# One output in three thirds: the channel mix of the first 256 tokens, with new order tables

## The chip, the cores and the metric

The kernel runs on one core of a Trainium2 chip. A core has a matrix engine (TensorE, PE in the profile), three engines for elementwise work (VectorE or DVE, ScalarE or ACT, GpSimd or POOL) and a queue engine (SyncE or SP) that issues most DMA transfers. Each engine takes its own instructions strictly in the order in which they were written; engines wait for each other by semaphores. The metric is the time of one execution on the device in microseconds; lower is better.

## What is computed

Three layers stand one behind the other, for 4 batches of 576 tokens and a width of 512. In the reference, cut to what matters:

```python
# attention, 8 heads of 64, causal in blocks of 64 tokens
scores = np.where(mask, scale * np.matmul(q, k.transpose(0, 1, 3, 2)), -1e9)
attn = np.exp(scores - np.max(scores, axis=-1, keepdims=True))
attn = attn / (np.sum(attn, axis=-1, keepdims=True) + 1e-09)
x = np.matmul(attn, v)                        # heads side by side: (4, 576, 512)
# channel mix
xk = mu_k * x + (1.0 - mu_k) * x_prev         # x_prev: x shifted by one token
xr = mu_r * x + (1.0 - mu_r) * x_prev
k = np.maximum(xk @ w_k, 0.0)                 # (512 -> 1024)
v = k * k @ w_v                               # (1024 -> 512)
x = 1.0 / (1.0 + np.exp(-(xr @ w_r))) * v     # w_r: 512 -> 512
# token and channel mixer
u = x + (np.maximum(x.transpose(0, 2, 1) @ w_tok1, 0.0) @ w_tok2).transpose(0, 2, 1)
out = u + np.maximum(u @ w_ch1, 0.0) @ w_ch2
```

## The kernel before, in words

A dense product is made of numbers split into an upper and a lower part, each of which TensorE multiplies exactly enough: w·x becomes wh·xh + wl·xh + wh·xl, three matmuls in place of one. Weights are split where they arrive, chunk by chunk, by `load_split`: a DMA loads a chunk (L345), ACT casts its top (L352), DVE joins (L355), ACT makes the upper part (L361) and POOL the lower part (L364). Chunks of w_r and w_k come first, those of w_v while the first batch is at work.

Work is cut into groups. `a{b}{hf}{pr}` is the attention of batch b, half hf and head pair pr; half 0 is the first 256 tokens (two blocks of 128 queries, j = 0 and 1), half 1 the other 320 (j = 2, 3 and, of 64 queries, 4). A unit of such a group and one j goes through scores (PE, L510), largest and bias (DVE, L544 and L553), exponentials (ACT, L563), their sums and inverse (DVE), the upper 16-bit part of the probabilities (`first`, ACT L587) and the lower (`second`, DVE L593), which both go to a tile pin, a transposing DMA on SP's queue (`turn`, L599), which makes the tile pt, and the products with v (`pv.products`, PE L646). Each pt tag, pt0 to pt4 for j = 0 to 4, has two buffers; where j < 4 a unit takes both, one for each head.

`c{b}{hf}` is the channel mix of one half. For each 128 of the 512 channels `mix` scales the shifted tokens (ACT L720), adds the others (DVE L726), and makes the upper part xh (L732, ACT or DVE) and the lower part xl (L736, POOL or DVE). Four `r_group`s, eight `k_group`s and four `v_group`s follow on PE: in an r or k output 8 matmuls with xh (both parts of the weight, L751) and then 4 with xl (L756), in a v output 16 and 8 with kh and kl. They add up in an accumulator of tag l, of which there are two; it comes free when `r_out` (ACT L792), `k_out` (ACT L820) or `v_out` (DVE) has read it. Squares of k are split into kh and kl (L845, L848). Before, all steps of an output wait for both parts of its weights (`need`) and for the parts of x that they read.

Then the last layer follows in groups `f{b}` and `b{n}` (L764 and others); its matmuls fill TensorE from about 400 us on.

The order of all of this is not that of the code. `Plan.schedule` lets each engine choose, among the steps that its model says are ready, the one with the smallest key; a step's key is its due time, less a number for its kind (table `lead_of`), less one for its group (table `shift`), and for the groups of the beginning (`begin`: the weights and the first batch's attention and mix) less one more for its kind (table `lead_begin`). The instructions are then written in that order.

## Time and profile before

| | us |
|---|---|
| median of 3 runs | 805.56 |
| lowest and highest run | 805.19, 806.23 |
| the profiled execution | 811.06 |
| its span, first to last instruction | 809.3 |
| busy in the span: PE | 763.7 |
| DVE | 477.3 |
| ACT | 419.2 |
| POOL | 181.3 |

The times are those of runs without the profiler, apart from the profiled execution, which was taken once and from which all views come. Its mean granted TensorE clock is 0.993 of full speed. The page divides the span in 40 slices; PE is busy 90% or more in nearly all slices but the first few and the last, and the other engines are busy half of the time and more in the first 400 us and little after that. How much of an engine's busy time matters is decided by stretches, and by what ended each wait, so the views by window and the timelines of single engines are used below. In a timeline a row joins like instructions that follow each other (x8); its second number is the time from the start of the first to the end of the last, and the number in brackets is the idle time ahead of it and what ended that.

### The profile page before, as it was taken

To read this page: it belongs to the slowest core of one execution; us is meant where nothing else is said; L and a number is where in the kernel's file an instruction comes from. 1 tells how busy PE (TensorE), PEld (TensorE's weight loads), DVE (VectorE), ACT (ScalarE), POOL (GpSimd) and SP (SyncE) were. 2 spreads that over 40 slices of the span, in tenths; PEclk is the share of its full clock that TensorE was granted. 3 is DMA by queue.
4 is the path that set the end of the run, shared out by engine and by line. 5 is a ranking of instruction groups with operands and counts; after the bars stand their busy time and mean duration, and the time that the engine had idled before them with its cause. 6 is when DMAs were issued, how large, how long until landed. Compare 5 with 4: busy or idle time off the path is not lost.

```text
span 809.3 us, 16129 instructions
## 1 busy us (share of the span) xinstructions
PE 763.7 (94%) x6120; PEld 661.7 (82%) x6120; DVE 477.3 (59%) x1194; ACT 419.2 (52%) x1070; POOL 181.3 (22%) x209
## 2 busy tenths in 40 slices
PE   2459999998999999999999999999999999999998
PEld 1227899887989999999999989998888888888886
DVE  7897898997798987789555687612212302301210
ACT  6887978687678795778564565502201201301100
POOL 3433524334145142432443222200000000000000
PEclk9999999999899999999999999999999999999999
DMA  8976964686465843566552654200000010000001
GB/s 272 269 189 106 201 148 115 146 170 120 113 138 125 159 117 93 117 140 113 191 180 84 232 170 141 78 27 1 14 26 1 14 39 14 1 26 14 14 13 40
DMA packets 136750, 84.30 MB, mean 104 GB/s; under 512 B 110944, under 2 KB 118240, under 8 KB 136160
## 3 DMA queue, kind: packets, MB, share of 16 engines
q1 hardware_dynamic: 136672, 83.27, 41.8%
q8 instruction: 48, 0.79, 0.4%
q14 instruction: 30, 0.25, 0.1%
HBM read 47.58 MB, written 9.44 MB: 70 GB/s over the span
## 4 chain that ended last, share of the span: by engine, by line
PE 81%; DVE 7%; DMA 5%; ACT 5%; issue 2%; SPq 0%; POOL 0%; ACTq 0%; DVEq 0%
PE b L764 37%; PE l L751 18%; PE l L756 9%; PE s L510 5%; PE o L646 4%; PE b L938 3%; PE b L959 3%; DMA pt<-pin 3%; DVE pin L593 2%; DMA wst<-in_w_k 1%; PE b L914 1%; DVE nm L544 1%; ACT pin L587 1%; ACT p L563 1%; DMA qkl<-in_w_v 1%
## 5 line engine op out<-in xcount | busy, mean ns | idle before, releaser
L1030 ACT ACTIVATE wy<-b 128x512 fp32r<-128x512 f32 (+1 forms) x60 | 33.3, 555 | 211.8 <-PE b L764 211.2
L764 PE MATMUL b<-uh,wx 128*128 128x512 f32 (+1 forms) x480 | 139.6, 373 | 0.0
L751 PE MATMUL l<-xh,wx 128*128 128x256 f32 (+1 forms) x768 | 123.7, 302 | 2.2 <-ACT r L792 1.8
L751 PEld LDWEIGHTS l<-xh,wx 128*128 128x128 f32 x768 | 107.9, 190 | 7.4 <-ACT r L792 2.0
L764 PE MATMUL b<-wy,c2a 128*128 128x512 f32 (+1 forms) x460 | 110.8, 367 | 0.0
L764 PEld LDWEIGHTS b<-uh,wx 128*128 128x128 f32 x480 | 87.2, 188 | 17.3 <-issue 0.2
L764 PEld LDWEIGHTS b<-wy,c2a 128*128 128x128 f32 x460 | 79.2, 189 | 15.3
L593 DVE SCALAR_TENSOR_TENSOR pin<-p,rs,pin 128x128 f16<-128x128 f32 (+4 forms) x112 | 77.0, 707 | 7.5 <-ACT pin L587 7.3
L1045 DVE TENSOR_TENSOR x<-b,x 128x256 f32<-128x256 f32 (+7 forms) x32 | 13.5, 454 | 114.8 <-PE b L764 114.8
L751 PE MATMUL l<-kh,wy 128*128 128x256 f32 (+1 forms) x512 | 78.1, 304 | 0.2 <-DVE ve L428 0.2
L646 PEld LDWEIGHTS <-vb 128*64 128x64 f16 x1920 | 52.9, 115 | 29.8 <-issue 13.7
L646 PE MATMUL o<-pt,vb 128*64 128x128 f16 (+1 forms) x1920 | 62.4, 220 | 14.3 <-DMA pt<-pin 7.2
L764 PE MATMUL b<-gx,wx 128*128 128x512 f32 x192 | 75.4, 393 | 0.0
L751 PEld LDWEIGHTS l<-kh,wy 128*128 128x128 f32 x512 | 71.5, 194 | 2.5 <-issue 1.4
L563 ACT ACTIVATE p<-s,nb 128x384 f32<-128x384 f32 (+4 forms) x112 | 61.6, 553 | 19.2 <-DVE nb L553 9.7
L587 ACT ACTIVATE pin<-p,rs 128x128 f16<-128x128 f32 (+4 forms) x112 | 63.2, 588 | 13.2 <-DMA pt<-pin 6.9
L756 PE MATMUL l<-xl,wx 128*128 128x320 f32 (+1 forms) x384 | 68.2, 300 | 0.0
L544 DVE TENSOR_REDUCE nm<-s 128x2 f32<-128x256 f32 (+4 forms) x80 | 63.6, 798 | 1.9 <-PE s L510 1.3
L756 PEld LDWEIGHTS l<-xl,wx 128*128 128x128 f32 x384 | 56.6, 190 | 2.1 <-issue 1.2
L1033 DVE SCALAR_TENSOR_TENSOR wy<-b,wy 128x512 fp32r<-128x512 f32 (+1 forms) x28 | 16.1, 576 | 62.8 <-ACT wy L1030 62.7
L1033 DVE SCALAR_TENSOR_TENSOR gx<-b,wy 128x512 fp32r<-128x512 f32 x32 | 21.9, 690 | 47.8 <-ACT wy L1030 47.8
L736 POOL TENSOR_TENSOR xl<-mt,xh 128x256 fp32r<-128x256 f32 (+1 forms) x32 | 28.4, 891 | 91.7 <-DVE xh L732 52.5
(116 smaller groups left out, 1397.0 us busy)
## 6 DMA issues: line engine op xcount, KB each, us to landing
wst<-in_w_c SPq DMA_DIRECT2D x24, 256.0 KB, 2.7
qkf<-in_kq SPq DMA_DIRECT2D x12, 480.0 KB, 3.5
v<-in_v SPq DMA_DIRECT2D x16, 320.0 KB, 3.1
x<-xd SPq DMA_DIRECT2D x4, 1152.0 KB, 7.0
wst<-in_w_c2a SPq DMA_DIRECT2D x18, 256.0 KB, 2.7
qkl<-in_w_v SPq DMA_DIRECT2D x16, 256.0 KB, 3.4
wst<-in_w_k SPq DMA_DIRECT2D x9, 410.0 KB, 5.4
qkf<-in_kq SPq DMA_DIRECT2D x12, 256.0 KB, 2.9
```

Of the source, the lines that this page charges most:

```text
L510: self.nc.tensor.matmul(o, q[e, q0:q0 + P], k[e, k0:k1], start=n == 0, stop=n == len(terms) - 1)
L544: nc.vector.tensor_reduce(out=c["nm"][:, :nh], in_=m, axis=AX.XY if j == 4 else AX.X, op=ALU.max, negate=True)
L563: nc.scalar.activation(out=c[x], in_=s, func=AF.Exp, scale=0.125, bias=c["nb"][:, x:x + 1], accum_out=c["sm"][:, x:x + 1],)
L587: nc.scalar.activation(out=like(pin[:, :n]), in_=c[x], func=AF.Copy, scale=rs)
L593: nc.vector.scalar_tensor_tensor(out=like(pin[:, w:w + n]), in0=c[x], scalar=rs, in1=like(pin[:, :n]), op0=ALU.mult, op1=ALU.subtract)
L646: nc.tensor.matmul(o[hh * D:hh * D + D, q0:q0 + rows], v[:, i, y, hh, :], st["pt", hh, j][:, x * (j + 1) + i, :], start=i == x == y == 0, ...
L736: (nc.vector if i in pl["xl_d"] else nc.gpsimd).tensor_tensor(out=l, in0=x[i], in1=raw(x["h"][i]), op=ALU.subtract)
L751: self.nc.tensor.matmul(ps, ww[:, k, :], x[0][k], start=k == 0 and n == 0, stop=False)
L756: self.nc.tensor.matmul(ps, w[0][:, k, :], x[1][k], start=False, stop=k == kt - 1)
L764: self.nc.tensor.matmul(ps, ww[k], xx[k], start=k == 0 and n == 0, stop=k == kt - 1 and n == 2)
L1030: nc.scalar.activation(out=gh(m), in_=d["g", m][:, :n], func=AF.Relu)
L1033: nc.vector.scalar_tensor_tensor(out=gl(m), in0=d["g", m][:, :n], scalar=0.0, in1=raw(gh(m)), op0=ALU.max, op1=ALU.subtract)
```

## The change

In group c00, the channel mix of the first 256 tokens of the first batch, every r, k and v output is made in three thirds, each a step of its own: wh·xh, wh·xl and, last, wl·xh. A third waits only for its own part of the weight and its own part of the input (`need` with `parts`). Before, wh·xh and wl·xh were interleaved and wh·xl came last. The number of matmuls is the same. All other groups are made as before.

```diff
+    def mm_one(self, ps, w, x, term, k0, k1, kt):
+
+        ww, xx = ((w[0], x[0]), (w[0], x[1]), (w[1], x[0]))[term]
+        for k in range(k0, k1):
+            self.nc.tensor.matmul(
+                ps, ww[:, k, :], xx[k], start=term == 0 and k == 0, stop=term == 2 and k == kt - 1
+            )
...
-            def r_group(i, k0, k1, xr=xr, c=c, n=n):
-                if k0 == 0:
+            def r_group(i, k0, k1, term=None, xr=xr, c=c, n=n):
+                if k0 == 0 and not term:
                     c["rp", i] = self.ps_l.tile([P, 512], F32, tag="l", name="l")
                 ps = c["rp", i][:, :n]
-                if k0 < KD:
+                if term is not None:
+                    self.mm_one(ps, self.wr[i], (xr["h"], xr["l"]), term, k0, k1, KD)
+                elif k0 < KD:
...
+            begin = b == 0 and hf == 0
+
+            def group(key, fn, i, x, name, ps):
+                if begin:
+                    for term in range(3):
+                        last = step("PE", c_pe(4 * n, 4), key, fn, i, 0, KD, term,
+                                    r=x["tl" if term == 1 else "th"] + self.need(name, i, (term // 2,)), w=[ps])
+                    return last
+                tok = self.need(name, i)
...
-                for k0 in range(0, NF + 1, 4):
+                for term, k0 in itertools.product(range(3), (0, 4)) if begin else ():
+                    step("PE", c_pe(4 * n, 4), key, v_group, i, k0, k0 + 4, term, after=[last],
+                         r=[(tkl if term == 1 else tkh, k) for k in range(k0, k0 + 4)] +
+                         self.need("wv", i, (term // 2,)), w=[ps])
+                for k0 in () if begin else range(0, NF + 1, 4):
...
     shift={
-        "a000": 194.57, "a001": -21.47, "a002": 2.43, "a003": 144.84, "a010": -1.55, "a011": -11.09, "a012": 1.1,
+        "a000": 194.57, "a001": -19.98, "a002": -5.02, "a003": 152.8, "a010": 1.41, "a011": -11.22, "a012": 1.1,
```

The functions `k_group` and `v_group` are changed like `r_group`. The tables `lead_of`, `shift` and `lead_begin` have new numbers, for nearly all kinds and groups, so the order changes on every engine from the first tens of microseconds to the end of attention and mix; from about 400 us on it is nearly the same. Three places show how.

On ACT, at the first `r_out`: l_864 and, after, l_779 are the accumulator of the first r output, qkl_731 and qkl_721 the same chunk of w_v. Before:

```order
L732 CAST xh_805<-mt_721 128x256
L720 ACTIVATE mt_854<-xt0_133,omu_62 128x256
L352 CAST tw1_64<-qkl_731 128x256
L361 CAST wy_72<-qkl_657 128x256
L655 ACTIVATE xt1_593<-o_742,vo_183 128x320
L720 ACTIVATE mt_878<-xt0_131,omu_62 128x256
L792 ACTIVATE r_891<-l_864 128x256
L563 ACTIVATE p_897,sm_896<-s_703,nb_893 128x384
```

After:

```order
L720 ACTIVATE mt_774<-xt0_135,omu_62 128x256
L720 ACTIVATE mt_784<-xt0_131,omu_62 128x256
L563 ACTIVATE p_788,sm_787<-s_707,nb_776 128x384
L361 CAST wy_72<-qkl_664 128x256
L587 ACTIVATE pin0_90<-p_702,rs_710 128x384
L802 ACTIVATE r_811<-l_779 128x256
L352 CAST tw1_64<-qkl_721 128x256
L563 ACTIVATE p_821,sm_787<-s_707,nb_776 128x384
```

`r_out` (L792, now L802) stood behind the cast of that chunk and now stands ahead of it.

On DVE, at the end of the mix of c00: the tiles xt0_129 to xt0_135 are the tokens of the four channel blocks, mt_770, mt_854 and mt_878 are the last three blocks of xk (after: mt_732, mt_774 and mt_784), and an xh is the upper part of the mt behind the arrow. Before:

```order
L726 SCALAR_TENSOR_TENSOR mt_770<-xt0_135,mu_60,mt_770 128x256
L726 SCALAR_TENSOR_TENSOR mt_854<-xt0_133,mu_60,mt_854 128x256
L736 TENSOR_TENSOR xl_933<-mt_735,xh_912 128x256
L732 CAST xh_941<-mt_770 128x256
L736 TENSOR_TENSOR xl_948<-mt_854,xh_935 128x256
L726 SCALAR_TENSOR_TENSOR mt_878<-xt0_131,mu_60,mt_878 128x256
L575 TENSOR_SCALAR rs_964<-sm_896 128x2
L575 TENSOR_SCALAR rs_966<-sm_920 128x2
L732 CAST xh_968<-mt_878 128x256
```

After:

```order
L575 TENSOR_SCALAR rs_946<-sm_860 128x2
L732 CAST xh_948<-mt_732 128x256
L581 RECIPROCAL rs_946<-rs_946 128x2
L544 TENSOR_REDUCE nm_955<-s_865 128x2
L593 SCALAR_TENSOR_TENSOR pin3_93<-s_726,rs_946,pin3_93 128x512
L593 SCALAR_TENSOR_TENSOR pin0_90<-s_726,rs_946,pin0_90 128x512
L553 TENSOR_SCALAR nb_1009<-nm_955 128x2
L355 SCALAR_TENSOR_TENSOR qkl_819<-qkl_819,tw0_63 128x256
L726 SCALAR_TENSOR_TENSOR mt_784<-xt0_131,mu_60,mt_784 128x256
L355 SCALAR_TENSOR_TENSOR qkl_921<-qkl_921,tw1_64 128x256
L732 CAST xh_1023<-mt_784 128x256
```

The last block of xk (mt_878 and xh_968, now mt_784 and xh_1023) now stands behind a reduction of scores, two pin subtractions and two joins, which all came after it before.

On SP, the turns of units a111 and a112 in the second batch. Before, pt3_3097 to pt4_3152 are a111's, pt2_3353 to pt3_3436 a112's. After, pt3_3111, pt3_3126 and pt4_3274 are a111's, pt2_3221, pt2_3248, pt3_3354, pt3_3415 and pt4_3441 a112's. Before:

```order
L599 DMA_TRANSPOSE pt3_3125<-pin1_91 128x8x128
L599 DMA_TRANSPOSE pt4_3152<-pin3_93 128x10x128
L487 DMA qkf_3280<-in_kq1 128x960
L599 DMA_TRANSPOSE pt2_3353<-pin2_92 128x6x128
L599 DMA_TRANSPOSE pt2_3399<-pin0_90 128x6x128
L599 DMA_TRANSPOSE pt3_3420<-pin1_91 128x8x128
L599 DMA_TRANSPOSE pt3_3436<-pin3_93 128x8x128
L487 DMA qkf_3509<-in_kq0 128x512
L599 DMA_TRANSPOSE pt0_3518<-pin2_92 128x2x128
```

After:

```order
L599 DMA_TRANSPOSE pt3_3126<-pin1_91 128x8x128
L487 DMA qkf_3149<-in_kq1 128x960
L599 DMA_TRANSPOSE pt2_3221<-pin0_90 128x6x128
L599 DMA_TRANSPOSE pt2_3248<-pin2_92 128x6x128
L599 DMA_TRANSPOSE pt4_3274<-pin3_93 128x10x128
L599 DMA_TRANSPOSE pt3_3354<-pin1_91 128x8x128
L487 DMA qkf_3408<-in_kq0 128x512
L599 DMA_TRANSPOSE pt3_3415<-pin0_90 128x8x128
L599 DMA_TRANSPOSE pt4_3441<-pin2_92 128x10x128
L599 DMA_TRANSPOSE pt1_3462<-pin3_93 128x4x128
```

The two pt2 turns of a112 came behind all of a111's turns and in one row with a112's pt3 turns; now they come ahead of a111's last turn, and a112's pt3 turns follow one by one.

## Rows read from the trace of the kernel before

**Rows 1.** The page, part 1: busy us, share of span, instructions

```profile
PE 763.7 (94%) x6120; PEld 661.7 (82%) x6120; DVE 477.3 (59%) x1194; ACT 419.2 (52%) x1070; POOL 181.3 (22%) x209
```

**Rows 2.** Windows: length, busy us (instructions) per engine, clock, DMA share, GB/s

```profile
75.00:100.00 25.00, 24.92 (x291) 21.16 (x290) 20.77 (x54) 22.68 (x60) 11.73 (x17) 1.00 0.78 167
...
200.00:240.00 40.00, 37.09 (x394) 34.17 (x393) 32.50 (x89) 28.09 (x77) 10.51 (x10) 0.91 0.60 125
...
400.00:760.00 360.00, 360.00 (x1919) 309.62 (x1918) 133.44 (x283) 105.23 (x239) 36.86 (x47) 1.00 0.20 65
```

**Rows 3.** Timeline of PE, r outputs, last v output: start us, us, instruction, idle

```profile
65.04 1.21 PE L751 MATMUL l<-xh,wx 128*128 128x256 f32 x8
...
66.56 1.11 PE L751 MATMUL l<-xh,wx 128*128 128x256 f32 x8
...
67.51 0.64 PE L756 MATMUL l<-xl,wx 128*128 128x256 f32 x4
...
69.90 1.56 PE L751 MATMUL l<-xh,wx 128*128 128x256 f32 x8 [1.76 <-ACT r L792]
...
74.04 1.13 PE L510 MATMUL s<-qk 64*128 64x512 f32 x4
...
75.67 1.11 PE L751 MATMUL l<-xh,wx 128*128 128x256 f32 x8
...
112.83 1.36 PE L751 MATMUL l<-kh,wy 128*128 128x256 f32 x10
```

**Rows 4.** Timeline of ACT at the first r_out

```profile
68.00 0.48 ACT L352 CAST tw<-qkl 128x256 f16<-128x256 bf16 x1 [3.62 <-DMA qkl<-in_w_v]
...
69.48 0.37 ACT L792 ACTIVATE r<-l 128x256 f32<-128x256 f32 x1
```

**Rows 5.** Timeline of DVE at the mix, 68 to 80 us

```profile
68.57 0.42 DVE L355 SCALAR_TENSOR_TENSOR qkl<-qkl,tw 128x256 uint32<-128x256 uint32 x1 [1.96 <-ACT tw L352]
...
73.90 0.29 DVE L732 CAST xh<-mt 128x256 fp32r<-128x256 f32 x1
...
75.28 0.17 DVE L538 MEMSET s<- 64x128 f32 x1 [0.59 <-PE s L510]
...
76.62 1.21 DVE L544 TENSOR_REDUCE nm<-s 128x2 f32<-128x1024 f32 x1
...
79.01 0.75 DVE L593 SCALAR_TENSOR_TENSOR pin<-s,rs,pin 128x512 f16<-128x512 f32 x1 [1.18 <-ACT pin L587]
...
79.67 0.61 DVE L593 SCALAR_TENSOR_TENSOR pin<-p,rs,pin 128x384 f16<-128x384 f32 x1
```

**Rows 6.** Windows behind stall A, columns as in rows 2

```profile
70.00:72.00 2.00, 2.00 (x12) 2.00 (x12) 1.73 (x5) 2.00 (x8) 0.74 (x1) 0.64 0.43 131
...
72.00:74.00 2.00, 2.00 (x10) 1.79 (x9) 1.49 (x6) 2.00 (x7) 0.73 (x1) 0.50 0.46 135
```

**Rows 7.** Timeline of PE around stall B

```profile
190.83 2.38 PE L646 MATMUL o<-pt,vb 128*64 128x128 f16 x96
...
201.91 1.86 PE L646 MATMUL o<-pt,vb 128*64 128x128 f16 x31 [2.82 <-DMA pt<-pin]
...
203.70 3.67 PE L751 MATMUL l<-kh,wy 128*128 128x256 f32 x16
```

**Rows 8.** SP's queue, turns of a112; all turns' landing, 186:203

```profile
191.72 6.52 SPq L599 DMA_TRANSPOSE pt<-pin  x4
...
DMA to landing us min/median/max: 2.8/3.5/4.9
```

**Rows 9.** Timeline of DVE, pins of the pt3 turns of a112

```profile
187.69 1.41 DVE L593 SCALAR_TENSOR_TENSOR pin<-p,rs,pin 128x512 f16<-128x512 f32 x2 [0.87 <-ACT pin L587]
```

**Rows 10.** Timeline of POOL: lower parts of weights and of x

```profile
50.01 1.06 POOL L364 TENSOR_TENSOR wx<-wst,wx 128x406 fp32r<-128x406 f32 x1 [2.57 <-ACT wx L361]
...
64.28 0.84 POOL L736 TENSOR_TENSOR xl<-mt,xh 128x256 fp32r<-128x256 f32 x1 [2.28 <-DVE xh L732]
...
106.06 0.74 POOL L364 TENSOR_TENSOR wy<-qkl,wy 128x256 fp32r<-128x256 f32 x1 [3.69 <-ACT wy L361]
```

More of the change, by code (lines that the diff above doesn't have):

```diff
@@ L61 @@
-        -14.49, "mix.low": 3.37, "mix.shifted": 147.07, "pv.products": -2.92, "pv.total": 92.69, "split_chunk.high":
-        -63.89, "split_chunk.join": 6.76, "split_chunk.load": 143.85, "split_chunk.low": 282.21, "split_chunk.top":
-        -112.45, "unit.bias": 105.96, "unit.exps": -239.76, "unit.first": -135.83, "unit.inverse": 471.77,
-        "unit.largest": 1.71, "unit.mask": -0.69, "unit.scores": 481.59, "unit.second": 298.83, "unit.sums": 7.56,
-        "unit.turn": -61.72,
+        "attention.edge": -690.11, "back.<lambda>": 64.01, "back.g_group": -21.39, "back.g_high": -731.07,
@@ L66 @@
+        -59.37, "split_chunk.join": 5.0, "split_chunk.load": 142.86, "split_chunk.low": 238.49, "split_chunk.top":
+        -112.56, "unit.bias": 108.62, "unit.exps": -255.19, "unit.first": -131.35, "unit.inverse": 475.23,
+        "unit.largest": 1.71, "unit.mask": -0.69, "unit.scores": 479.08, "unit.second": 303.17, "unit.sums": 7.56,
+        "unit.turn": -68.08,
     },
     shift={
[8 rows of a table removed]
[8 rows of a table added]
     },
@@ L91 @@
-        19.35, "mix.low": 63.96, "mix.shifted": 223.54, "pv.products": -1.86, "pv.total": 4.3, "split_chunk.high":
-        191.37, "split_chunk.join": -2.04, "split_chunk.load": -58.89, "split_chunk.low": -104.87, "split_chunk.top":
-        225.28, "unit.bias": 146.72, "unit.exps": 56.02, "unit.first": 220.91, "unit.inverse": -61.06, "unit.largest":
-        0.1, "unit.mask": 86.57, "unit.scores": 187.42, "unit.second": -42.99, "unit.sums": -11.55, "unit.turn":
+        "attention.edge": 435.9, "back.<lambda>": 51.92, "back.g_group": -195.96, "back.g_high": -56.18, "back.g_low":
@@ L95 @@
+        191.37, "split_chunk.join": -2.47, "split_chunk.load": -54.54, "split_chunk.low": -124.73, "split_chunk.top":
+        225.28, "unit.bias": 137.27, "unit.exps": 56.02, "unit.first": 220.91, "unit.inverse": 37.71, "unit.largest":
+        0.1, "unit.mask": 90.54, "unit.scores": 188.62, "unit.second": -43.91, "unit.sums": -11.55, "unit.turn":
         -135.86,
@@ L327, in load_split, with need @@
         return key + dt * -(-n // size)
-    def need(self, name, i):
+    def need(self, name, i, parts=(0, 1)):
         block, size = self.cover[name]
-        return [(name, (c, y)) for c in range(i * block // size, -(-(i + 1) * block // size)) for y in range(2)]
+        return [(name, (c, y)) for c in range(i * block // size, -(-(i + 1) * block // size)) for y in parts]
     def split_chunk(self, key, stage, src, part, k, tok, gate, top_v, high_v, low_v):
```

61 lines of the change are left out of this document (32 added, 29 removed), and 14 rows, old and new, of the table shift.

## The prediction

> **What bounds the kernel now.** I read the page first: TensorE (PE) computes for 763.7 us of the 809.3 us span [rows 1], so at most 45.6 us could be won by feeding it better. The busy time by stretches [rows 2] says where those lie. From 75 us on PE hardly stops (24.92 of 25 us, and 360.00 of 360 in the late part), with one hole between 200 and 240 us. Most of the rest lies ahead of 68 us, where the kernel loads and splits weights and begins attention, and there the change alters little. Two stalls of PE stand inside the reach of the change, so I went on to the timelines of the engines around them.
>
> Stall A, in the first channel mix. PE makes the first two r outputs at 65.04 to 67.99 and then stands 1.76 us, since the third needs the accumulator that the first holds until `r_out` has read it [rows 3]. `r_out` was late because ScalarE (ACT) takes its work in order: ahead of it stood a cast of a chunk of w_v (L352) for which ACT stood 3.62 us [rows 4]. VectorE (DVE) stood 1.96 us behind the same cast [rows 5]. When PE resumes, its granted clock is 0.64 and then 0.50 for two stretches of 2 us [rows 6], that is, mostly the lower of its two levels, 1.2 GHz. The price of the slow stretch: from 69.90 to 74.04 PE did 20 matmuls; at the pace of 8 in 0.95 us (66.56 to 67.51) they need 2.38 us, so 1.76 us more are gone [rows 3]. Stall A costs 3.5 us.
>
> Stall B, in the second batch's attention. At 201.91 PE has stood 2.82 us for the second of the two transposed tiles on tag pt3 of unit a112 [rows 7]. Then 31 small matmuls take 1.86 us where 96 had taken 2.38, so about 1.1 us too long, and 16 matmuls take 3.67 us where two runs of 8 take 0.95 + 1.11 [rows 3], 1.6 us too long. Stall B costs 2.8 + 1.1 + 1.6, about 5.4 us. Its cause is seen on the queue that issues transposes: the four turns of a112 begin at 191.72 and fill 6.52 us [rows 8], although DVE had written the operands of the pt3 turns from 187.69 to 189.1 [rows 9]. Each pt tag has two buffers, a unit uses both, and they come free when the products of the unit before, a111, have read them; those stood in one run of 96 at 190.83 to 193.15 [rows 7].
>
> **The change, part by part.**
>
> 1. The thirds themselves. An output keeps its 12 matmuls (v: 24), so PE's own work is the same. What could be won is the wait for the lower part of a weight. No such wait is there: the last lower part of w_r and w_k is made by GpSimd (POOL) at 50.01 to 51.07, 14 us ahead of the first r output; the last of w_v ends at 106.80 [rows 10], 6 us ahead of the last v output (112.83, [rows 3]). Removing nothing gives 0. It adds something small: the third with x's lower part now stands second, 0.5 us after the start instead of 1 us. x's lower part takes POOL 0.84 us [rows 10] after the upper part is there, so up to 0.4 us once at the first r output; that lies ahead of a longer wait (step 3) and I count 0.
>
> 2. The tables move instructions on all engines from about 36 us on. In front of stall A, `r_out` of the first output now stands ahead of the cast that waited (the order of ACT), so the 1.76 us of PE and most of the 1.96 us of DVE go. The last upper part of xr comes 1.8 us of DVE's work earlier, so the r outputs begin at about 62.5 instead of 65.04.
>
> 3. But the second part of the mix pays. Ahead of the last upper part of xk (DVE L732, at 73.90 now, [rows 5]) DVE gets a score reduction (1.13 to 1.21 us), four pin subtractions (two of 0.6 and two of 0.75 us), a join (0.4 us) and small ones: 4.4 us of work [rows 5]. From 73.90 that is 78.3; less the 1.96 us of idle time that goes, 76.3; plus the waits for ACT's pins that come with the work (0.6 and 1.18 us, [rows 5]), 78.1. I take 77.5. The first k output can start at 77.8, against 75.67 now. PE has by then 1.9 us more work behind it than now at its first k output (attention products were drawn ahead), so by work alone it is 77.8 - 75.67 - 1.9 = 0.2 us late. From 62.5 on PE has about 10 us of work before it (four r outputs at 1.43 us, 96 products at 2.38 us, two groups of scores), and the fourth r output must wait until `r_out` of the second is through, about 70.5; so PE is done at about 73.5 and stands some 4 us. After the 1.76 us of stall A it ran slow for 1.76 us [rows 3]; after 4 us I expect the same price. Sum of the early part, against a present time that includes stall A: 0.2 + 1.76 = +2.0 us. Ends: xk at 76.3 and no slow stretch, 76.6 - 75.67 - 1.9 = -1.0; xk at 78.5 and a slow stretch as long as B's (2.6 us), 78.8 - 77.6 + 2.6, about +3.8.
>
> A rule of the Trainium skill, TensorE: Matmul & The Clock Gate, section "HAM oscillation — how this bites in real kernels", speaks against this step: a stream of matmuls that stops for its operands starts again at half clock each time, so that the stop costs more than its length. By the rule the step is +2.0, without it +0.2; rows 3 and 6 agree with the rule at both stalls.
>
> 4. Stall B. The products of a111 no longer stand in one run: those on pt2 move 6.8 us of PE's work earlier, those on pt3 1.4 us, so a112's two pt2 turns are free to go well before and no longer queue in front of the pt3 turns. Between the products of a111 and of a112 on pt3, PE now has 7.8 us of work instead of 6.9, on pt2 12.6 instead of 6.7. The last pt3 operand of a112 is written some 2.6 us of DVE's work later, about 192; with one turn (about 1.6 us each now, 6.52 over 4) and a landing in 2.8 to 4.9 us [rows 8] it is there by 196.5 to 198.5, and PE arrives at about 198. I count the whole 5.4 us as gone. Ends: 0 (a new wait of the same kind, on pt3 or pt4, in its place) and -5.6.
>
> 5. The order of PE changes kind (products of pv, scores, dense groups) 14 times more often. A run of 8 dense matmuls takes 1.21 us behind another kind and 1.11 behind its own [rows 3]: 14 x 0.1 = +1.4 us, all on the path since PE is the bound; I take 1.3. Ends 0 and 2.8 (double, if the way in costs as much as the way out).
>
> 6. The late part, 400 us on, has the same order; PE is 100% busy there [rows 2]. 0.
>
> Sum: 0 + 2.0 - 5.4 + 1.3 = -2.1 us. The profiled execution took 811.06 us (span 809.3 and 1.8 around it) and would take 809.0. It stands 5.5 us above the median of the runs, 805.56; taken from that, 803.5.
>
> **The rivals.**
>
> Slower: a wait takes the place of stall B. If the pt3 turn of a112 still lands after PE's arrival, or the fourth-block tile pt4, now read directly behind pt3, does, PE stands again and restarts slow; the early part and the kind changes then stand alone: 805.56 + 2.0 + 1.3 = 808.9. It decides at landing times of about 5 us and more, and the last one now took 4.9 behind a full queue [rows 8]. It would be so too if the timed runs had less of stall B than the profiled one, which is 5.5 us longer than they are. For it speaks that all the margins in step 4 are about 1 us; against it, that the bunch of four turns is broken up.
>
> No change: stall B goes, but the wait ahead of the k outputs reaches its upper end: -5.4 + 3.8 + 1.3 = -0.3, 805.3.
>
> Larger gain: xk comes at its early end, so that stall A is won and nothing paid, and the kind changes cost little: -5.4 - 1.0 + 0.3, 799.5. For it: DVE and ACT lose their common wait of 2 and 3.6 us. Against: the 4.4 us are real work on an engine that is nearly full there.
>
> The thirds do nothing by themselves in any of these; that part of the change "doesn't do what it says" is in my view certain, and what decides is the order.
>
> **How the numbers follow.** Two runs of this kernel can be told apart at about 0.2%, 1.6 us: faster is below 803.95, slower above 807.17. Chances: forecast (803.5, its own range 802.2 to 804.8) 0.38; larger gain 0.17; no change 0.19; slower 0.26. The forecast's own range lies about seven tenths below 803.95, so faster gets 0.27 + 0.17 = 0.44; same the other 0.11, and most of no change, 0.28; slower 0.28 with the tail of no change. The range takes in all cases but their outer tails: 799.0 to 809.0.
>
> **What would show it.** In the profile after: an idle time of PE of about 4 us, ended by DVE xh L732, ahead of the first k output near 77.8, with a granted clock near 0.6 behind it; no wait of ACT at L352 ahead of the first `r_out`; in the stretch 190 to 210 us no wait of PE on pt above 0.5 us and a clock of 1.00. Wrong would be: PE waiting for a lower part of a weight, which this trace doesn't have; a new wait on pt of over 2 us anywhere from 80 to 400 us; a late part longer than now.

## The result: slower, by 6 us

The changed kernel takes 812.11 us (median of 4 runs, 811.17 to 813.10) against 805.89 us (805.19 to 806.39): a ratio of 1.0078 with a 95% interval of 1.0060 to 1.0095, or 4.8 to 7.7 us more. The forecast was 803.5 us with a range of 799.0 to 809.0; the time lies outside it, and on the other side of no change.

The profile after is that of an execution of 811.17 us with a span of 809.4 us. The profile before had a span of 809.3 us, from an execution of 811.06 us. Put beside each other, the two pages show hardly any difference, and that is the first finding: the execution that I read before is not like most of those that were timed. Its 811.06 us stand above each of the 101 timings of that kernel beside the result and the experiments (802.75 to 810.83 us). Of the 97 beside the experiments, the 70 with a mean granted clock of 0.999 or 1.00 have a median of 805.4 us and the 27 with 0.993 to 0.998 one of 808.3 us, and the profiled execution, with 0.993, belongs to the latter. The changed kernel took 811.81 and 811.17 us with clocks of 0.999 and 1.00, so its loss is not one of the clock.

The kernel before was run again with a profile of its own (`before_again`, below, an execution of 806.56 us), and where the text says "the second profile before", it means that one.

The page of after, part 1 (busy us, share of the span, instructions), answers to [rows 1]:

```profile
PE 761.3 (94%) x6120; PEld 657.3 (81%) x6120; DVE 477.5 (59%) x1194; ACT 420.7 (52%) x1070; POOL 180.3 (22%) x209
```

By stretches, as in [rows 2] (length, busy us and instructions of PE, PEld, DVE, ACT, POOL, granted clock, DMA share, GB/s), first of after:

```profile
57.00:100.00 43.00, 39.46 (x498) 31.49 (x498) 36.54 (x99) 38.93 (x102) 15.39 (x21) 1.00 0.87 169
100.00:140.00 40.00, 37.51 (x392) 33.46 (x391) 35.86 (x100) 32.69 (x99) 15.07 (x17) 1.00 0.59 144
200.00:300.00 100.00, 98.53 (x1121) 89.29 (x1121) 85.33 (x235) 78.31 (x214) 34.58 (x37) 1.00 0.62 130
300.00:400.00 100.00, 99.19 (x1189) 91.98 (x1184) 78.92 (x206) 72.25 (x180) 33.52 (x38) 1.00 0.54 118
```

and of the second profile before:

```profile
57.00:100.00 43.00, 41.75 (x504) 33.71 (x501) 37.16 (x97) 38.22 (x102) 18.42 (x24) 1.00 0.89 171
100.00:140.00 40.00, 39.37 (x405) 35.49 (x403) 35.16 (x104) 33.32 (x103) 15.24 (x16) 1.00 0.54 127
200.00:300.00 100.00, 96.39 (x1132) 87.56 (x1131) 88.07 (x236) 80.83 (x222) 32.97 (x33) 1.00 0.63 132
300.00:400.00 100.00, 99.17 (x1127) 93.55 (x1126) 76.36 (x196) 69.91 (x173) 34.01 (x38) 1.00 0.56 132
```

The rows show where PE stands longer: 43.00 - 39.46 = 3.5 us against 1.3 at 57 to 100 us, 2.5 against 0.6 at 100 to 140, and, the other way round, 1.5 against 3.6 at 200 to 300 us. Behind that the stretches are equal in standing time, and still lose a little: PE takes longer for the same work. To see the balance, each matmul was counted at the usual distance to the next of its form, and the work done by a moment was compared. What PE of the changed kernel is behind the second profile before (an estimate: with other choices of these distances the value at 300 us comes out between 1.2 and 3.3 us):

```
at us         60    80   100   120   140   160   200   220   260   300   340   400   600   end
behind, us   0.7   2.4   3.1   3.2   5.1   5.3   4.7   4.6   2.8   2.3   4.1   3.9   4.9   4.6
```

So there are three losses (up to 100 us, 120 to 140 us and, with a size that is less sure, behind 300 us) and one gain of about 2.4 us between 200 and 300 us, where the second profile before has waits that the changed kernel has not (0.84 us at 209.81 and 1.28 us at 237.85 are the longest).

The timeline of PE of after at the r and k outputs (start, length, instruction, idle time ahead and what ended it) answers to [rows 3]:

```profile
58.12 0.32 PE L646 MATMUL o<-pt,vb 128*64 128x128 f16 x2 [2.65 <-ACT vb L443]
...
65.29 0.75 PE L762 MATMUL l<-xh,wx 128*128 128x256 f32 x4
...
67.86 1.08 PE L646 MATMUL o<-pt,vb 128*64 128x128 f16 x32
...
69.94 0.82 PE L646 MATMUL o<-pt,vb 128*64 128x64 f16 x40
...
75.59 1.24 PE L510 MATMUL s<-qk 128*128 128x288 f32 x4 [0.52 <-DVE pin L593]
...
76.45 1.34 PE L762 MATMUL l<-xh,wx 128*128 128x256 f32 x8
...
127.06 1.46 PE L751 MATMUL l<-xh,wx 128*128 128x320 f32 x8 [1.39 <-ACT r L802]
```

and at the pv products of a111 and a112, [rows 7]:

```profile
192.99 1.08 PE L646 MATMUL o<-pt,vb 128*64 128x128 f16 x32
...
195.14 0.82 PE L646 MATMUL o<-pt,vb 128*64 128x64 f16 x40
...
200.13 0.86 PE L646 MATMUL o<-pt,vb 128*64 128x128 f16 x24
...
201.47 1.72 PE L646 MATMUL o<-pt,vb 128*64 128x128 f16 x72
```

No wait of PE for a pt tile of a112 is left there, as step 4 said. But the same place in the second profile before, and its first r outputs, look like this:

```profile
61.74 3.27 PE L646 MATMUL o<-pt,vb 128*64 128x128 f16 x96
...
64.94 1.22 PE L751 MATMUL l<-xh,wx 128*128 128x256 f32 x8
...
69.89 1.21 PE L751 MATMUL l<-xh,wx 128*128 128x256 f32 x8 [0.40 <-ACT r L792]
...
72.67 1.11 PE L751 MATMUL l<-xh,wx 128*128 128x256 f32 x8
...
197.14 1.05 PE L646 MATMUL o<-pt,vb 128*64 128x128 f16 x31 [0.36 <-DMA pt<-pin]
...
198.13 2.17 PE L751 MATMUL l<-kh,wy 128*128 128x256 f32 x16
```

Ahead of the third r output PE does not wait at all, where it stood 1.76 us; it waits 0.40 us ahead of the fourth (69.89). The wait for the last pt3 tile is 0.36 us, not 2.82 (197.14), and the matmuls behind both run at the pace of those ahead (16 in 2.17 us, not 3.67). Neither wait is longer than half a microsecond there.

The queue that the prediction blamed for stall B stands in the second profile as well. Its row answers to [rows 8], and so does the row on the landing of all turns at 186 to 203 us:

```profile
189.69 5.58 SPq L599 DMA_TRANSPOSE pt<-pin  x4
...
DMA to landing us min/median/max: 2.3/3.5/3.5
```

The queue is 0.9 us shorter than in the first profile (5.58 against 6.52), and the tile that PE waits for lands 3.1 us after its issue (193.99 to 197.10), where it took 4.9 us (196.96 to 201.86). So of the 2.5 us by which the two waits differ, the longer landing makes up most.

### The profile page after: what moved, and what is told of

Its sections match the earlier page's. It is cut to its first block, busy times and chain, and to the rows that moved or that the text cites. A ratio compares the mean times of both kernels' runs of the same rounds, so it can differ in the third digit from the quotient of the medians.

```text
span 809.4 us, 16123 instructions
## 1 busy us (share of the span) xinstructions
PE 761.3 (94%) x6120; PEld 657.3 (81%) x6120; DVE 477.5 (59%) x1194; ACT 420.7 (52%) x1070; POOL 180.3 (22%) x209
## 4 chain that ended last, share of the span: by engine, by line
PE 67%; ACT 2%; DVE 1%; issue 0%; DMA 0%; POOL 0%; ACTq 0%; POOLq 0%
PE b L772 37%; PE l L751 11%; PE l L756 6%; PE b L964 3%; PE b L985 3%; PE o L646 2%; PE s L510 2%; PE b L940 1%; ACT pin L587 0%; ACT p L563 0%; DVE pin L593 0%; DMA v<-in_v 0%; ACT kt L840 0%; DVE nm L544 0%; DVE x L1071 0%
## 5 line engine op out<-in xcount | busy, mean ns | idle before, releaser
L751 PE MATMUL l<-xh,wx 128*128 128x320 f32 (+1 forms) x672 | 109.2, 302 | 1.8 <-ACT r L802 1.4
L751 PEld LDWEIGHTS l<-xh,wx 128*128 128x128 f32 x672 | 94.7, 188 | 6.7 <-ACT r L802 1.7
L593 DVE SCALAR_TENSOR_TENSOR pin<-p,rs,pin 128x128 f16<-128x128 f32 (+4 forms) x112 | 81.6, 744 | 8.1 <-ACT pin L587 7.4
L646 PEld LDWEIGHTS <-vb 128*64 128x64 f16 x1920 | 50.8, 114 | 25.1 <-issue 11.1
L646 PE MATMUL o<-pt,vb 128*64 128x128 f16 (+1 forms) x1920 | 60.3, 218 | 9.8 <-DMA pt<-pin 4.5
L751 PE MATMUL l<-kh,wy 128*128 128x320 f32 (+1 forms) x448 | 68.0, 302 | 0.9 <-DVE r L903 0.4
L751 PEld LDWEIGHTS l<-kh,wy 128*128 128x128 f32 x448 | 61.9, 189 | 3.3 <-issue 1.0
L756 PE MATMUL l<-xl,wx 128*128 128x320 f32 (+1 forms) x336 | 59.9, 300 | 0.0
L756 PEld LDWEIGHTS l<-xl,wx 128*128 128x128 f32 x336 | 49.5, 188 | 1.3 <-issue 0.6
L510 PE MATMUL s<-qk 64*128 64x128 f32 (+4 forms) x80 | 25.6, 678 | 24.1 <-ACT p L563 18.8
```

The costliest lines, as they stand in the source:

```text
L510: self.nc.tensor.matmul(o, q[e, q0:q0 + P], k[e, k0:k1], start=n == 0, stop=n == len(terms) - 1)
L593: nc.vector.scalar_tensor_tensor(out=like(pin[:, w:w + n]), in0=c[x], scalar=rs, in1=like(pin[:, :n]), op0=ALU.mult, op1=ALU.subtract)
L646: nc.tensor.matmul(o[hh * D:hh * D + D, q0:q0 + rows], v[:, i, y, hh, :], st["pt", hh, j][:, x * (j + 1) + i, :], start=i == x == y == 0, ...
L751: self.nc.tensor.matmul(ps, ww[:, k, :], x[0][k], start=k == 0 and n == 0, stop=False)
L756: self.nc.tensor.matmul(ps, w[0][:, k, :], x[1][k], start=False, stop=k == kt - 1)
```

## The experiments

All kernels but one build the plan of their kernel as it is and then write its steps out by a fixed list of their numbers instead of by `Plan.schedule`:

```diff
     def run(self):
-        order = self.schedule()
-        for s in order:
-            s.fn(*s.args)
+        replay(self)      # for n in ORDER: self.steps[n].fn(...)
```

With the list that the schedule itself gives, every engine has the instructions of the kernel in the same order, so an edit of the list is an edit of the order and of nothing else. Theories: **O**, the loss lies in the new order, and the stalls belong to one execution; **L**, the stalls are in every run and the loss lies where the two profiles don't show it; **S**, the thirds themselves cost.

**The kernel before again.** No edit.

> The kernel before, unchanged, with a profile of its own. Theory O (the loss is in the new order, and the two us-long stall B of the first profile, 5.4 us at 199 to 207 us, belongs to that one execution and not to the timed runs): a profile with a span near 804 us and no wait of PE on pt above 1 us near 200 us; ratio 1.000. Theory L (stall B is in every run, and the loss of the change lies somewhere that the two profiles don't show): span near 809 us with the stall of 2.8 us there again.

Ratio 1.0012 (0.9995 to 1.0029), 10 runs from 803.76 to 809.65 us; the profile has a span of 804.8 us and the rows above. On ACT the cast which it stood 3.62 us for in [rows 4] is there 2 us earlier:

```profile
65.83 0.49 ACT L352 CAST tw<-qkl 128x256 f16<-128x256 bf16 x1 [1.52 <-DMA qkl<-in_w_v]
```

The load of the w_v chunk landed at 65.8 us and not at 68.0. Theory L is out, since the stalls are not in every run; by the clocks of the runs above, PE spends some time at the lower clock in about one run in four, and such a stall may be the reason. The two spans differ by 4.5 us, while the prediction priced the two stalls at 3.5 + 5.4 = 8.9 us. So even in the execution that it was read from, about half of that price was given back (an estimate from the two spans): behind stall B the first profile waits 0.38 us and nothing where the second has its 0.84 and 1.28 us.

**The thirds alone, and the order alone.** For the first, the list of before with the three steps of an r or k output of c00 replaced by the thirds; for the second, the list of after with the thirds replaced by the old steps.

```diff
-ORDER = before:  ... r_group(0, k 0:2), r_group(0, k 2:4), r_group(0, low) ...
+ORDER = before:  ... r_group(0, wh*xh), r_group(0, wh*xl), r_group(0, wl*xh) ...
```

> The three thirds alone: the instructions of every engine stand in the order of the kernel before, and only in group c00 each 12 matmuls of an r or k output are done as wh*xh, wh*xl, wl*xh in the places of the old three steps (v outputs: 4, 8 and 12 matmuls in the three places). Theory O: 805.9, within 1 us, since no weight was waited for. Theory S (the thirds themselves cost, by the earlier wait for x's lower part in each output or by their form): 808 or more.

> The new order alone: the instructions of every engine stand in the order of the changed kernel, and in group c00 the outputs are made as before (both weight parts with x's upper part first, then the lower part of x). Theory O: 812, within 1 us. Theory S: 806 to 808.

The thirds alone: 808.25 us, ratio 1.0021 (1.0003 to 1.0039). The order alone: 813.32 us, ratio 1.0092 (1.0072 to 1.0113). So the loss is in the order. What the thirds do is small either way: they add 0.2 to 3.1 us to the old order, and the new order is as slow without them as with them (1.0092 against 1.0078, with overlapping intervals). In the traced execution of the thirds alone PE keeps level with the second profile before up to 200 us (within 0.4 us, by the count above), far behind the last third. Its loss of 1.6 us comes from one wait for a score buffer, where that profile waits 0.84 us, and from slow matmuls behind it (a granted clock of 0.60 from 211 to 215 us):

```profile
211.35 0.50 PE L510 MATMUL s<-qkh 64*128 64x512 f32 x2 [2.62 <-DVE pin L593]
```

**Which part of the order.** Lists that take the first steps from one kernel and all others, in their order, from the other (always with the thirds). In the first of the expectations below, the 1.3 and 3.3 us are counted against the first profile before, and not, as in the table above, against the second.

```diff
-ORDER = before
+ORDER = after[:650] + [n for n in before if n not in after[:650]]      # after_to_99
```

> The changed kernel's first 650 steps of the plan in their order (to about 99 us: all of attention of the first batch's first half and most of its second, the r and k outputs and most v outputs of c00), then all other steps in the order of the kernel before. Theory O with the loss spread (PE was 1.3 us behind at 100 us and 3.3 at 130, compared by matmuls done): 807, that is 1 to 2 us lost. Theory O with all of the loss made early: 811 to 812. Theory S: 811 to 812.

> The order of the kernel before for the first 400 steps of the plan (to about the first r outputs, 64 us), thirds in place, then all others in the order of the changed kernel. If the early loss is made before the first r output (theory V): 809 to 810, the early 2 to 3 us are gone and the later loss stays. If it is made in the mix itself, behind 64 us, as the prediction's step on xk said: 812.

> The order of the kernel before for the first 650 steps (to about 99 us), thirds in place, then all others in the order of the changed kernel. What the changed order costs behind 99 us alone: by the lag of PE in the traces about 1 to 2 us more than split_only, 808 to 810; if all of the loss is made before, 806 to 808.

> The changed order for its first 1050 plan steps (to about 160 us), then the order of the kernel before. PE stood 5 us behind at 160 us in the changed kernel. Theory P (PE is the bound from 75 us on, so what it is behind stays): 810 to 811. Theory E (elastic: PE in the kernel before stands 3.6 us between 200 and 300 us, which a PE that comes later doesn't, so part of the loss is given back): 807 to 809.

> The order of the kernel before to about 160 us (1050 steps, thirds in place), then the changed order. Theory P: 806 to 807 (PE gains 2.5 us between 200 and 300 us and loses some 2.6 behind 300). Theory E: with the gain between 200 and 300 us only there for a late PE, 808 to 809.

> The changed order to about 296 us (1950 steps), then the order of the kernel before. PE was 2.4 us behind there in the changed kernel: 808 to 809 if the rest of the loss (1.7 us more of dense-to-other switching at 300 to 400 us, 0.7 us in the late part) goes with the old order; 812 if that rest is only variation between executions.

> The order of the kernel before to about 296 us (thirds in place), then the changed order: 808 to 809 if the changed order costs 2.4 us behind 300 us (9 more switches of kind on PE there, and one wait of 0.5 us on a back group); 806 if it doesn't.

> The changed order for its first 400 plan steps (about 64 us), then the order of the kernel before. If the early 2.4 us are lost ahead of the first r output: PE 2 us behind at 80 us and 807 to 808 in the end. If they are lost in the mix: no lag at 80 us and 806.

```
list                               median   ratio    95% interval
changed order to  64 us, then old  807.53   1.0018   1.0002 to 1.0035
changed order to  99 us, then old  812.00   1.0058   1.0039 to 1.0077
changed order to 160 us, then old  810.22   1.0069   1.0042 to 1.0095
changed order to 296 us, then old  816.59   1.0139   1.0110 to 1.0168
old order to  64 us, then changed  812.83   1.0086   1.0062 to 1.0111
old order to  99 us, then changed  813.36   1.0090   1.0056 to 1.0124
old order to 160 us, then changed  811.58   1.0064   1.0040 to 1.0087
old order to 296 us, then changed  809.04   1.0039   1.0012 to 1.0067
```

All eight have the thirds, so what their order adds is to be measured against the thirds alone (1.0021). The eight don't add up, and the traces say why: a list has a seam, the place where it changes from one order to the other, and there something is missing that either order alone had prepared. The waits of PE at the seams of three of them:

```profile
104.89 0.33 PE L510 MATMUL s<-qkh 64*128 64x128 f32 x2 [2.62 <-ACT qkh L491]
```

```profile
169.56 0.44 PE L510 MATMUL s<-qkh 64*128 64x384 f32 x2 [2.43 <-ACT p L563]
```

```profile
316.50 3.56 PE L751 MATMUL l<-kh,wy 128*128 128x256 f32 x16 [3.86 <-DVE r L903]
```

Old to 99 us has 2.62 us for a key tile, old to 160 us 2.43 us for a score buffer, and changed to 296 us 3.86 us for an accumulator with slow matmuls behind (16 in 3.56 us). These three, and old to 64 us, which loses at 70.84 and 78.13, tell nothing on the place of the loss. The four others have no such wait at their seam:

- Changed to 64 us: +0.2 to +2.8 us, no more than the thirds alone. In its trace, which is that of the fastest of its ten runs, PE waits the same 2.65 us for v as the changed kernel and is 1.1 us behind at 80 us and 1.6 at 140, but by 300 us all of that is given back, and the span (804.6 us) is no longer than that of the second profile before. So a lag made ahead of the first r output is not shown to cost anything in the end.
- Changed to 99 us: seven runs, 808.03, 808.48 and 809.05, and four from 812.00 to 812.44. The first three, with clocks of 0.999 to 1.00, are no slower than the thirds alone; the four have 0.989 to 0.995. The profile is of one of the latter and has stall B again, to 0.01 us at the same time and length as in [rows 7]:

```profile
190.92 2.38 PE L646 MATMUL o<-pt,vb 128*64 128x128 f16 x96
...
201.91 1.87 PE L646 MATMUL o<-pt,vb 128*64 128x128 f16 x31 [2.83 <-DMA pt<-pin]
```

- Changed to 160 us: PE is 4.9 us behind at 160 and 3.2 us at 300 and at the end. So 1.7 us are given back, and behind 300 us the old order loses nothing more, where by the count the changed one lost 2.3.
- Old to 296 us, then changed: +1.0 to +5.4 us. Against the thirds alone (1.0039 against 1.0021, overlapping intervals) it is not shown that the changed order costs anything behind 296 us, and its trace, that of the slowest of its ten runs, can't decide it.

Beyond the thirds, then, the first 64 us of the new order add nothing that can be seen, the first 99 us nothing in three runs and nearly 4 us in four, and the first 160 us some 2 us by the medians (the intervals, 1.0042 to 1.0095 and 1.0003 to 1.0039, do not overlap). So a part of the loss is made between 64 and 160 us; the rest is not placed.

**The v of the fourth head pair.** PE of the changed kernel waits 2.65 us for it (58.12, above). Its v is late because its buffer is that of the third pair's v, whose scaling comes later in the changed order. Edits: these steps at their old places in the changed order, and at their new places in the old order.

```diff
-ORDER = after
+ORDER = after, load_v.{power .. two} of pair 3 and load_v.* of pair 4 at before's places
```

> The changed kernel, except that the steps which scale v for the third and fourth head pair of the first batch (power, gather, the four small steps, both parts of v, and the load of the fourth pair's v, which shares one buffer with the third's) stand on DVE, ACT, PE and SP at the places that the kernel before gives them. Theory V (early loss: these steps come 3 to 4 us late, PE stands for the fourth pair's v at 58 us and the r outputs start with 72 products less behind them): 809.5, that is 2 to 3 us of the loss come back. Theory W (DVE and ACT are full up to 62 us, so the order of these small steps doesn't matter; the loss comes from what else was drawn ahead): 812.

> The order of the kernel before with the thirds in place (as in split_only), except that the same v steps of the third and fourth head pair stand at the later places that the changed kernel gives them. Theory V: 2 to 3 us more than split_only, 809 to 811. Theory W: as split_only, 807 to 808.

Early: 812.51 us, ratio 1.0084 (1.0065 to 1.0103), nothing gained. Late: 808.15 us, 1.0034 (1.0009 to 1.0060), against 1.0021 for the order that it was made from, within the intervals. Neither decides on theory V. The intervals of the late list leave room for its 2 us, though in its trace PE waits 1.68 us for that v and the span (804.6 us) is still that of the second profile before. And the early list does not bring the fourth pair's v forward: ACT starts on it at 56.73, against 57.23 in the changed kernel and 54.19 before. One of the steps ahead of it stands on POOL (L416), which the edit left at its place, behind a lower part of x that waits for its upper part:

```profile
54.47 0.72 POOL L736 TENSOR_TENSOR xl<-mt,xh 128x256 fp32r<-128x256 f32 x1 [2.48 <-DVE xh L732]
55.17 0.37 POOL L416 TENSOR_SCALAR vd<-eye,vm 128x128 bf16<-128x128 bf16 x1
```

On PE, the trace of v_early shows these waits:

```profile
47.66 2.29 PE L510 MATMUL s<-qk 128*128 128x288 f32 x4 [5.89 <-ACT p L563]
...
53.20 1.65 PE L510 MATMUL s<-qk 64*128 64x384 f32 x4 [1.83 <-ACT p L563]
...
57.61 0.32 PE L646 MATMUL o<-pt,vb 128*64 128x128 f16 x2 [1.76 <-ACT vb L443]
...
66.07 1.02 PE L762 MATMUL l<-xh,wx 128*128 128x256 f32 x4
```

The third pair's v is there 3 us earlier, but the waits for scores, for which ACT has to be done with an older unit (5.89 and 1.83 us), are together no shorter than in the changed kernel (5.13 and 2.12), the fourth pair's v is still waited for (1.76), and the r outputs begin at 66.07, later than there.

**The two stalls, each attacked alone in the old order.**

```diff
 # PE                                          # ACT
+a111 pv.products(2)                           +c00 r_out(0)
 c10 k_group(4, low)                            wv  split_chunk.top
 ... three more dense steps, one of scores      wv  split_chunk.high
 c10 k_group(5, low)                            a010 pv.total
-a111 pv.products(2)                            c00 mix.shifted
 a111 pv.products(3)                           -c00 r_out(0)
```

> The kernel before, except that on PE the products of unit a111 on pt2 stand 5 steps (some 3 us) earlier, so that the two pt2 buffers come free before the products on pt3 and pt4, and the four turns of a112 need not queue up. The prediction's step 4 (stall B is in every run): 800 to 802. Stall B only in some executions: a median within 1 us of before, and fewer runs at 808 and above.

> The kernel before, except that on ACT the first r_out stands ahead of the cast of the w_v chunk that it waited behind. The prediction's reading of stall A (3.5 us in every run): 802 to 803. Stall A mostly a late landing in one execution (0.4 us of wait in the second profile): within 0.7 us of before.

pv_early: 805.79 us, ratio 0.9996 (0.9981 to 1.0012), one of 11 runs at 808 or above, against 7 of 33 runs of the kernel before beside it. In its profile a112's four turns still stand in one row, begun at 187.74 and not at 189.69, and PE doesn't wait for pt there; the median does not move, and the interval leaves room for a gain of 1.5 us at most. r_out_first: 806.93 us, 1.0018 (0.9998 to 1.0037), no gain and perhaps a small loss. There the wait was not taken away but passed on: the first r_out is early and the third r output does not wait, but the fourth waits for the second r_out, longer than the 0.40 us of the second profile before:

```profile
70.08 1.21 PE L751 MATMUL l<-xh,wx 128*128 128x256 f32 x8 [1.23 <-ACT r L792]
```

So stall B was worth 1.5 us at most in the median run, and moving the first r_out gains 0.2 us at most.

**Changes of kind on PE.** The changed order has 14 more. Added to the old order, and taken from the new one, by exchanging neighbours on PE.

```diff
-pv(2)  pv(3)  k_group          # old order, at 8 places: 14 more changes
+pv(2)  k_group  pv(3)
...
-k_group  scores  k_group  pv   # changed order, at 10 places
+k_group  k_group  scores  pv
```

> The kernel before, with its own order on all engines but PE; there, at 8 places behind 75 us where two pv products of one unit stand in a row ahead of a dense step, the dense step is put between them. PE changes kind 14 times more often, as in the changed kernel, and nothing else moves. The prediction's step 5 (0.09 to 0.1 us for each change of kind): 807, +1.3 us. At the price which the traces suggest behind 300 us (1.7 us for 9 changes): 808.2, +2.6. If a change of kind costs nothing: 805.6.

> The changed kernel, except that on PE, at 10 places behind 75 us where one step of another kind stands between two dense steps and another such step follows, the two neighbours change places. That takes away 14 changes of kind, as many as the change added. If a change of kind costs PE 0.1 to 0.17 us (the traces, and the same number added to the old order cost 2.3 us in the median): 809.5 to 811, 1.3 to 2.3 us less than the changed kernel's 812.1. If the cost in that run came from its shifted waits and not from the changes: 812.

Counted in the traces, the first has 14 changes more than the kernel before and the second 12 fewer than the changed one, not 14. Added: 808.12 us, ratio 1.0028 (1.0003 to 1.0053), 0.2 to 4.3 us. Taken away: 813.13 us, 1.0067 (1.0040 to 1.0093), nothing won. The first agrees with the prediction's +1.3. The second shows nothing of it, but its interval overlaps that of the changed kernel and leaves room for a gain of that size. And the waits of more_switches have grown as well (1.96 us at one score group, 1.6 us at the start of a late group). So the price of a change of kind by itself stays open.

**The wait for r_out at 125.7 us.**

```diff
 # ACT, changed order
+c01  r_out(1)
 a113 load_qk.high
-c01  r_out(1)
```

> The changed kernel, except that on ACT the second r_out of the first batch's second half (group c01) stands ahead of the cast of a key tile (L491) whose load ACT waits for, in place of behind it. PE waits 1.39 us for that r_out at 125.7 us in the changed kernel's profile. If that wait is a loss of its own: 811, about 1 us less. If PE waits for the next thing instead, or makes it up between 200 and 300 us: 812.

811.88 us, ratio 1.0061 (1.0044 to 1.0079) against 1.0078 (1.0060 to 1.0095): not to be told apart. In its profile PE still waits 0.96 us there for r_out. Moving this one step does not free the accumulator early enough, and no more can be said.

## Why the prediction was wrong, point by point

**Step 4 (stall B, -5.4 us) failed, and with it the sign.** Its mechanism is in the trace: where the products of a111 are spread, a112's turns no longer stand in one row and PE doesn't wait (after); begun earlier, they cause no wait in one row either (pv_early). But its size was read from one execution. In `before_again` the same queue costs 0.36 us with a granted clock of 1.00, since the last turn lands after 3.1 us and not 4.9, and taking the stall away alone moves the median by -0.04% (-0.19 to +0.12%). The prediction had seen that the profiled execution stood 5.5 us above the median of the runs, and named what that could mean ("if the timed runs had less of stall B than the profiled one"), but carried the difference of 5.5 us over to both sides instead of asking which part of the profile it was. It was nearly the size of the term. Without step 4 the sum of the prediction was +3.3 us; measured are +6.2.

**Step 2 (stall A) failed in the same way.** The 1.76 us and the slow stretch behind them come from a load that landed at 68.0 us; in the second profile it landed at 65.8 and PE waited 0.40 us. `r_out` stands ahead of the cast in the changed order, as forecast, and PE does not wait for it, but r_out_first shows that this alone gains 0.2 us at most, since the next r_out is waited for instead. Also wrong was the start of the r outputs at 62.5 us: it was worked out from DVE alone, and PE was not free. It came from two waits, 2.65 us for v and 0.57 us for scores, to 65.29 (before 64.94), and with 72 pv products less behind it than before, which it then does between the r outputs (67.86 and 69.94).

**Step 3 was wrong in its mechanism, and its size agrees with the loss by luck.** xk was late as forecast: the last cast to xh on DVE starts at 76.59, against 73.90 in [rows 5], where the step put it at 77.5 with an early end of 76.3.

```profile
76.59 0.29 DVE L732 CAST xh<-mt 128x256 fp32r<-128x256 f32 x1
```

The first k output starts at 76.45 (forecast 77.8), 3.8 us later than the 72.67 of the second profile before, with 1.9 us more work behind it: 1.9 us lost. The sum had +2.0, but counted from 75.67, the start in the first profile, which has stall A in it. From there the changed kernel comes out at 76.45 - 75.67 - 1.9 = -1.1 us, the early end of the step. The same steps counted from 72.67, without the slow restart, would have been 77.8 - 72.67 - 1.9 = +3.2 us, and with step 5's +1.3 and nothing for stall B +4.5 in all (an estimate from these rows): the sign of the result, and 1.7 us less than it. PE does not stand 4 us for xk, nor run slow behind: it was late itself, waits 0.52 us ahead of a score group, and its granted clock is 1.00 from 65 us on. By the rule of the Trainium skill that the prediction weighed (TensorE: Matmul & The Clock Gate, section "HAM oscillation — how this bites in real kernels") the loss would have been idle time with a slow restart; the rule had nothing to work on, since the idle time did not come. It can be seen at work in after_to_99, where the stretch from 195 to 205 us, with its wait of 2.83 us, has a clock of 0.80:

```profile
195.00:205.00 10.00, 7.03 (x89) 6.42 (x88) 6.08 (x18) 7.17 (x24) 5.54 (x5) 0.80 0.78 139
```

Three readings of the prediction are also off, with little weight in the sum. The first two r outputs ended at 68.14 us (69.90 less 1.76), not 67.99. The 0.59 us in [rows 5] that step 3 takes for a wait for ACT's pin is one for PE's scores. And the slow stretch behind stall B, which the sentence on the rule places in rows 3 and 6, is in rows 2 and 7.

**Step 1 held.** No PE wait of the changed kernel names a lower part of a weight, and the thirds alone gain nothing: they cost 0.2 to 3.1 us, in the one trace of them 100 us behind their place.

**Step 5 (14 changes of kind, +1.3 us) is not settled.** Behind 300 us PE of the changed kernel does its work with the same standing time (0.81 against 0.83 us) and takes 1.7 us more for it by the count, with 9 more changes; more_switches has 0.2 to 4.3 us for 14; fewer_switches shows no gain for 12 fewer.

**Step 6 (late part, 0) was off by 0.7 us.** In the changed order one of the last layer's groups stands directly behind another, and PE waits once where it did not wait before; a longer late part was one of the prediction's signs of being wrong:

```profile
552.51 0.50 PE L772 MATMUL b<-uh,wx 128*128 128x512 f32 x1 [0.52 <-DVE x L1071]
```

**What the prediction did not have** is the loss of 2 us at 120 to 140 us (waits of 1.39 and 0.41 us, against two of 0.21) and the one behind 300 us. It costed the places where the old profile showed a wait and took the rest of a new order on every engine as neutral. The runs speak against that, though not strongly. Of the fifteen orders that were run beside the old and the changed one, 13 are slower than the old by their interval, r_out_first is slower or the same, and pv_early is the same; none is faster. But 12 of the 13 carry the thirds as well, and three of these (changed to 64 us, old to 296 us, v_late) are not told apart from the thirds alone.

**The rivals.** The one on the slower side (808.9 us) had the right reason in its second half and the wrong one in its first: no new wait on pt took the place of stall B, but the timed runs did have less of it than the profiled one. Its time is still 3 us short of the measured one. It had a chance of 0.26; since the profiled execution stood above the timed runs by the size of the term, it should have been the forecast.

What is shown is that the loss comes with the new order and not with the thirds. What stays open is which of its steps make it. The lag begins ahead of 64 us, but the list that has only this part of the new order is no slower than the thirds alone. The v of the fourth pair was never brought forward, so it is not ruled out, and moving one `r_out` gained nothing. DVE and ACT are busy 85 to 91% of the time from 57 to 100 us in both orders, which is why I think that a repair often passes PE to the next wait; r_out_first shows it for one repair, and no run shows it for all.

## What to carry to other kernels

Before a term is taken from a profile, set the profiled execution against the timed runs: when it is slower by about the size of a stall in it, that stall may be an accident of its transfers, and removing it may win nothing in the median; a second profile of the same kernel settles this for little, and so does the granted clock of the timed runs, where it is on record. Both stalls here went back to a DMA that landed late, and had PE at the lower clock behind them. Count every term from the same execution: here the early part was counted from a start with a stall in it. And when a change comes with a new order on all engines, the places that the old trace shows as waits are no balance: the new order has waits of its own. In this kernel, with its nearly full engines, no other order that was tried was faster.

## What was not expected of the hardware

The same program on the same inputs differs by 8 us between executions (802.75 to 810.83 us over 101 runs), and PE's rows in the traces of two of them agree within 0.1 us from 45 to 67 us, until one load lands 2.2 us later. In two different kernels, both some 2 us late at 190 us, stall B came back with the same start and length to 0.01 us (201.91, 2.82 and 2.83 us): it looks less like noise than like one of two ways in which the transfers can fall, and the two groups of runs of changed to 99 us (808 to 809 us with clocks of 0.999 to 1.00, and 812 us with 0.989 to 0.995) would fit that. A trace of the lower group was not taken, and what decides was not tried.

Early in the program a granted clock of 1.00 in a view can mean that there is no record of the clock. The records begin at 64.8 us in the trace of after and at 63.6 us in the second profile before; a window ahead of them reads 1.00. In after_to_160, which has the order of after up to there, they begin at 50.6 us. Its rows show what the others leave out, first of after_to_160:

```profile
50.00:54.00 4.00, 1.30 (x12) 0.54 (x9) 3.46 (x11) 1.99 (x5) 1.67 (x3) 1.00 0.94 275
54.00:64.00 10.00, 4.92 (x33) 2.46 (x32) 8.66 (x25) 8.29 (x20) 2.34 (x4) 0.50 0.82 190
```

```profile
52.50 0.92 PE L510 MATMUL s<-qk 64*128 64x384 f32 x4 [2.12 <-ACT p L563]
```

and of after:

```profile
54.00:64.00 10.00, 5.07 (x35) 2.57 (x33) 8.67 (x25) 8.35 (x20) 2.30 (x5) 1.00 0.83 192
```

```profile
52.44 1.65 PE L510 MATMUL s<-qk 64*128 64x384 f32 x4 [2.12 <-ACT p L563]
```

The same four matmuls behind the same wait take 0.92 us where the clock is on record as 1.00, and 1.65 us where it is not on record. So PE probably runs at the lower of its two levels (1.2 of 2.4 GHz) there: in after_to_160 it does so from 54 to 64 us, by the 0.50 of that window. Which part of the early loss comes from a later rise of the clock (64.8 us against 63.6) was not tried.
